# A mixture-of-experts stage: weights in three groups of four parts, and scatters without order

## The chip, the cores and the metric

One core of a Trainium2 chip runs the whole program. The metric is the device time of one execution in microseconds (us); lower is better. The engines are TensorE (PE, with its weight loads shown as PEld), VectorE (DVE), ScalarE (ACT), GpSimd (POOL) and SyncE (SP, which here only issues DMAs).

## What is computed

A sliding-window attention, a gated feed-forward layer and a routed mixture of experts follow one another over 2304 tokens of 512 channels. The change touches the last one only:

```python
def _moe2_ref(x, w_skip, w_gate, w1, w2):          # w1 (8, 512, 1024), w2 (8, 1024, 512)
    out = x.copy()
    do_compute = x @ w_skip > 0
    xc = x[do_compute]
    ...                                            # e_idx: best expert of a token; gate_w: its softmax share
    for e in range(8):
        mask = e_idx == e
        h = np.maximum(xc[mask] @ w1[e], 0.0)
        y[mask] = gate_w[mask, None] * (h @ w2[e])
    out[do_compute] = xc + y
    return out
```

## The kernel before

**Stages.** Attention and the first feed-forward layer run over five blocks of tokens. As each block ends, its tokens go to DRAM (`x1d`, and as a first value to `out`) and are routed. The expert stage, `moe2`, starts when the last block is done, at about 571 us; its first weight loads start at about 545 us.

**Tiles.** Tokens of one expert are gathered in tiles of 128 rows. Each expert has up to two tiles here (s = 0 and 1); whether the second exists is known only on the chip, so PE's work on a second tile stands in a branch (`taken`). With these inputs the experts at places 0, 4 and 6 of the order have a second tile. The largest expert is put first, and one of its tiles is computed early, before the loop (`mm1(0, ...)`, `mm2(0, ...)`, `put(0, ...)`). More tiles than two would run in a loop at the end, which these inputs don't enter.

**Arithmetic.** Products are made in float32r with a high and a low part: each weight part is loaded raw (512 KB), ACT casts the high part (L862, L871), and a subtraction makes the low part (L863 on DVE for w1; L873 for w2, on DVE for parts 1 and 3 and on POOL for parts 2 and 4). Three products for each pair then make 24 matmuls of 512 columns for mm1 (w1) and 24 for mm2 (w2) of one tile.

**One tile's way.** `gather` (POOL) fetches the rows; `tx` turns them on PE into one of two PSUM buffers `tps` and copies them out as `xt`, high part on ACT (L906), low part on DVE (L907); `mm1` fills `hps`; `relu` makes `hr` (half on ACT L918, half on DVE L922); `th` turns `hr` through the same two `tps` buffers and copies it out as `ht` (ACT L933, DVE L934); `mm2` (L943) fills the accumulator `yps[s]`, one for each s; `put` makes `o` on DVE (L949) and scatters its rows into `out` with an indirect DMA that POOL issues (L950). The framework knows only that all scatters write `out`, and keeps them in order: each waits for the one before to land.

**Weights.** An expert's w1 has four parts, and so has its w2. `load_weights(e)` loads all eight, through five raw buffers (`rp`), on SP's queue in the order written. w1 turns in six buffers (`wp1`), w2 in six (`wpx` with two, `wpy` with four): one and a half experts each.

**Order.** Loop round i works on expert e = i: it loads the weights of the next expert, gathers the tokens of the one after, turns the next expert's first tile, does mm1 of e, then mm2 of the expert before (`last`), with transposes between. So mm2 of an expert runs one round after its mm1. The framework's planner then orders the instructions of every engine anew, by the order written and by when it expects their inputs; a branch moves only as a whole. Each engine then works through its queue strictly in that order.

**Memory.** The pools of `moe2` lie over those of the stage before, whose buffers come free one after the other until that stage ends.

Of the kernel before, what the change touches and what calls it, by code (L numbers as in the profile page):

```python
# [8 lines left out]
F32R = mybir.dt.float32r  # L9
# [6 lines left out]
P = 128  # L16
# [810 lines left out]
def moe2(ctx, tc, ph, ps_a, ctab, ident, x1d, ls, cnt, perm, permi, slot0, xg0, w1, w2, out):  # L827
    nc = tc.nc
    NT, DM = out.shape
    KD = DM // P  # L830
    FF = w1.shape[2]
# [12 lines left out]
    def pool(name, bufs, space=None):  # L844
        kw = {"space": space} if space else {}
        return ctx.enter_context(tc.tile_pool(name=name, bufs=bufs, reuse_waits="tile", **kw))

    wp1, rp, wpx, wpy = pool("wp1", 6), pool("rp", 5), pool("wpx", 2), pool("wpy", 4)
    xtp, mt, xp, hp_ = pool("xtp", 3), pool("mt", 1), pool("xp2", 2), pool("hp2", 2)
    n_w2 = [0]  # L850
    ps_h0 = pool("ps_h0", 1, bass.MemoryType.PSUM)
    ps_t = pool("ps_t", 1, bass.MemoryType.PSUM)
    ps_y = [pool(f"ps_y{s}", 1, bass.MemoryType.PSUM) for s in range(2)]
    ps_h1 = pool("ps_h1", 1, bass.MemoryType.PSUM)

    def load_weights(e):
        r1, r2 = [], []
        for c in range(4):
            raw = rp.tile([P, FF], F32, tag="raw", name="raw1")
            nc.sync.dma_start(out=raw, in_=w1[bass.ds(e, 1), c * P:(c + 1) * P, :].rearrange("o p f -> (o p) f"))  # L860
            w = wp1.tile([P, 2, FF], F32R, tag="w1", name="w1s")
            nc.scalar.copy(out=w[:, 0], in_=raw)  # L862
            nc.vector.tensor_tensor(out=w[:, 1], in0=raw, in1=w[:, 0].bitcast(F32), op=ALU.subtract)  # L863
            r1.append(w)
        for c in range(4):
            raw = rp.tile([P, 2, DM], F32, tag="raw", name="raw2")
            src = w2[bass.ds(e, 1), c * 2 * P:(c + 1) * 2 * P, :]
            nc.sync.dma_start(out=raw, in_=src.rearrange("o (two p) d -> p (o two) d", p=P))
            w = (wpx if n_w2[0] % 6 < 2 else wpy).tile([P, 2, 2, DM], F32R, tag="w2", name="w2s")
            n_w2[0] += 1  # L870
            nc.scalar.copy(out=w[:, 0], in_=raw)  # L871
            eng = nc.gpsimd if c in (1, 3) else nc.vector
            eng.tensor_tensor(out=w[:, 1], in0=raw, in1=w[:, 0].bitcast(F32), op=ALU.subtract)  # L873
            r2.append(w)
        return r1, r2

    hps = [(ps_h0, ps_h1)[s].tile([P, 2, FF // 2], F32, tag="h", name=f"hps{s}") for s in range(2)]
    tps = [ps_t.tile([P, 4, P], F32, tag=f"t{s}", name=f"tps{s}") for s in range(2)]
# [2 lines left out]
    def tp(src, yes=None):  # L881
        ps = tps[n_t[0] % 2]
        n_t[0] += 1
        with yes or ExitStack():
            for c in range(4):
                nc.tensor.transpose(ps[:, c], src[:, c * P:(c + 1) * P], ident)
        return ps
# [15 lines left out]
    def tx(xg, yes=None):  # L903
        ps = tp(xg, yes)
        xt = xtp.tile([P, 2, KD, P], F32R, tag="xt", name="xt")
        tx_last[0] = nc.scalar.copy(out=xt[:, 0], in_=ps)  # L906
        tx_last[1] = nc.vector.tensor_tensor(out=xt[:, 1], in0=ps, in1=xt[:, 0].bitcast(F32), op=ALU.subtract)  # L907
        return xt

    def mm1(s, xt, w, hs=(0, 1)):  # L910
        for h in hs:
            for n, (c, a, b) in enumerate(ORDER1):
                nc.tensor.matmul(hps[s][:, h], lhsT=xt[:, a, c], rhs=w[c][:, b, h * 512:(h + 1) * 512],  # L913
                                 start=(n == 0), stop=(n == 3 * KD - 1))

    def relu(s, both=False):
        hr = hp_.tile([P, 2, FF // 2], F32, tag="hr", name="hr")
        nc.scalar.activation(out=hr[:, 0], in_=hps[s][:, 0], func=AF.Relu)  # L918
        if both:
            nc.scalar.activation(out=hr[:, 1], in_=hps[s][:, 1], func=AF.Relu)  # L920
        else:
            nc.vector.tensor_scalar(out=hr[:, 1], in0=hps[s][:, 1], scalar1=0.0, scalar2=None, op0=ALU.max)  # L922
        return hr

    def th(hr, yes=None):
        pss = []
        with yes or ExitStack():
            for h in range(2):
                pss.append(tp(hr[:, h]))
        ht = hp_.tile([P, 2, KF, P], F32R, tag="ht", name="ht", bufs=3)  # L930
        for h in range(2):
            ps = pss[h]
            nc.scalar.copy(out=ht[:, 0, 4 * h:4 * h + 4], in_=ps)  # L933
            nc.vector.tensor_tensor(out=ht[:, 1, 4 * h:4 * h + 4], in0=ps,  # L934
                                    in1=ht[:, 0, 4 * h:4 * h + 4].bitcast(F32), op=ALU.subtract)
        return ht

    def mm2(s, ht, w, cs=range(8)):
        n = 3 * cs[0]
        for c0 in range(cs[0], cs[-1], 4):  # L940
            for a, b in PASSES:
                for c in range(c0, c0 + 4):
                    nc.tensor.matmul(yps[s], lhsT=ht[:, a, c], rhs=w[c // 2][:, b, c % 2],  # L943
                                     start=(n == 0), stop=(n == 3 * KF - 1))
                    n += 1

    def put(s, xg, slot):
        o = hp_.tile([P, DM], F32, tag="o", name="o", bufs=4)
        nc.vector.scalar_tensor_tensor(out=o, in0=yps[s], scalar=slot[2], in1=xg, op0=ALU.mult, op1=ALU.add)  # L949
        nc.gpsimd.indirect_dma_start(  # L950
            out=out, out_offset=bass.IndirectOffsetOnAxis(ap=slot[1].bitcast(U32), axis=0),
            in_=o, in_offset=None, bounds_check=NT - 1, oob_is_err=False)

    def slot_at(i):
        return gi[:, i:i + 1], si[:, i:i + 1], ls[:, 1, i:i + 1]

    wts, xg, xt, hr, ht = {}, {}, {}, {}, {}
    def expert(i):
        return nc.values_load(permi[0:1, i:i + 1], engines=(ET.SP,), min_val=0, max_val=NE - 1,
                              skip_runtime_bounds_check_because="an index of an expert")  # L960

    wts[0] = load_weights(expert(0))
    mm1(0, tx(xg0), wts[0][0])
    mm2(0, th(relu(0, True)), wts[0][1])
    put(0, xg0, slot0)

    gi = mt.tile([P, SLOTS], I32, name="gi")
# [22 lines left out]
    def taken(e, s):  # L990
        return tc.If(tiles_of[e] > 1) if s else ExitStack()

    def stage_g(e):
        for s in range(2):
            if (e, s) in slots:
                xg[e, s] = gather(slots[e, s], f"{e}_{s}")

    def stage_x(e, s):
        if (e, s) in slots:
            xt[e, s] = tx(xg[e, s], taken(e, s) if TX else None)  # L1000

    def stage_1(e, s, hs=(0, 1)):
        if (e, s) in slots:
            with taken(e, s):
                mm1(s, xt[e, s], wts[e][0], hs)
            if hs[-1] == 1:
                hr[e, s] = relu(s)

    def stage_t(e, s):
        if (e, s) in slots:  # L1010
            ht[e, s] = th(hr[e, s], taken(e, s) if TH else None)

    def stage_2(e, s, cs=range(8)):
        if (e, s) in slots:
            with taken(e, s):
                mm2(s, ht[e, s], wts[e][1], cs)
            if cs[-1] == 7:
                put(s, xg[e, s], slots[e, s])

    order = [*range(NE), None, None]  # L1020
# [3 lines left out]
    with tc.issue_after(si_last.ins):  # L1024
# [10 lines left out]
        le = mt.tile([1, 2, NU, NE], F32, name="le")  # L1035
# [26 lines left out]
    last = None  # L1062
    for i, e in enumerate(order[:-1]):
        nxt = order[i + 1]
        if i == 0:
            with tc.issue_after(tx_last[0].ins), tc.issue_after(tx_last[1].ins):
                wts[nxt] = load_weights(expert(nxt))
        elif nxt is not None:
            wts[nxt] = load_weights(expert(nxt))
        stage_g(order[i + 2] if i + 2 < len(order) else None)  # L1070
        if nxt is None:
            stage_1(e, 0)
            stage_t(last, 1)
            stage_1(e, 1)
            stage_2(last, 0, range(4))
            stage_t(e, 0)
            stage_2(last, 0, range(4, 8))
            stage_t(e, 1)
            stage_2(last, 1)
            stage_2(e, 1)  # L1080
            stage_2(e, 0)
            break
        stage_x(nxt, 0)
        stage_1(e, 0, (0,))
        stage_1(e, 1)
        stage_t(last, 1)
        stage_1(e, 0, (1,))
        stage_2(last, 0, range(4))
        stage_x(nxt, 1)
        stage_2(last, 0, range(4, 8))  # L1090
        stage_t(e, 0)
        stage_2(last, 1)
        last = e
    with tc.If(n_extra > 0):
        with tc.For_i(0, n_extra) as u:
            le, la = extra_regs(bass.ds(u, 1), (ET.SP,), (ET.DVE,))
            lw = load_weights(le)
            lslot = pick(la)
            lx = gather(lslot, "loop")
            lxt = tx(lx)  # L1100
            mm1(0, lxt, lw[0])
            lht = th(relu(0))
            mm2(0, lht, lw[1])
            put(0, lx, lslot)


_OUT = (2304, 512)
# [33 lines left out]
```

## Time and profile before

| | |
|---|---|
| time, median of 3 runs | 758.83 us (758.09 to 758.84) |
| time of the profiled execution | 758.27 us |
| its span | 756.5 us |
| PE busy | 715.5 us (95%) |
| DVE busy | 503.5 us (67%) |
| ACT busy | 327.3 us (43%) |
| POOL busy | 86.4 us (11%) |
| raw expert weights | 64 loads of 512 KB, 5.0 us from issue to landing (median) |

The span runs from the first to the last instruction that the profile shows; the time has some 1.8 us around it. Busy time is that of an engine at work on data; waiting, branching and issuing is not counted. Where an engine sat idle before an instruction, the profile names what ended that: the instruction, or the DMA, that released it.

### The profile page before, as it was taken

Reading aid. Unit: us, or ns where it says so; the run is one execution under the profiler, and the core shown is the slowest. Engines: PE = TensorE matmul, PEld = TensorE weight load, DVE = VectorE, ACT = ScalarE, POOL = GpSimd, SP = SyncE. Lnnn points to the kernel's source line nnn. Section 1 sums busy time; section 2 is a strip of 40 time slices with the busy share of each in tenths; the row PEclk is TensorE's granted clock in tenths of the full one; section 3 lists DMA queues with packets and bytes.
Section 4 is the critical chain, followed back from the end, with each engine's and each line's share of the span. In section 5 each row is a group of like instructions: output and inputs, shape, how many; then the busy total and the mean of one; then the engine's idle time right before and its main releaser. Section 6 shows DMA issues by size and latency. Waiting matters only on the chain. (4 is left out here: it accounts for less than half of the span.)

```text
span 756.5 us, 12268 instructions
## 1 busy us (share of the span) xinstructions
PE 715.5 (95%) x4456; PEld 580.6 (77%) x4456; DVE 503.5 (67%) x1122; ACT 327.3 (43%) x758; POOL 86.4 (11%) x65
## 2 busy tenths in 40 slices
PE   6699999999999999999999999999989999899994
PEld 4587778788878787878887888889887777677772
DVE  3988899858944549954457963523865676876662
ACT  5858667634333143233233213212143366765550
POOL 2100000000000000000000000000011416545342
PEclk9999999999999999999999999999999999999998
DMA  9795878775432416414416311116394667967531
GB/s 230 184 229 169 243 236 263 218 219 186 112 99 71 112 58 194 111 56 112 112 57 193 100 56 56 57 58 221 113 396 146 208 196 231 300 229 260 176 134 42
DMA packets 118163, 121.85 MB, mean 161 GB/s; under 512 B 76463, under 2 KB 89135, under 8 KB 118098
## 3 DMA queue, kind: packets, MB, share of 16 engines
q1 hardware_dynamic: 113794, 108.32, 47.9%
q0 software_dynamic: 2720, 6.92, 2.8%
q10 hardware_dynamic: 1584, 5.77, 2.1%
q8 instruction: 38, 0.62, 0.3%
q14 instruction: 27, 0.22, 0.1%
HBM read 102.78 MB, written 20.20 MB: 163 GB/s over the span
## 5 line engine op out<-in xcount | busy, mean ns | idle before, releaser
L411 PE MATMUL po<-wo,h 128*128 128x512 f32 x648 | 160.6, 392 | 2.2 <-DMA wo<-wo_hl 2.2
L387 PE MATMUL g<-xh,wgv 128*128 128x512 f32 (+1 forms) x496 | 152.3, 373 | 4.0 <-DVE th L393 2.2
L387 PE MATMUL v<-xh,wgv 128*128 128x512 f32 (+1 forms) x496 | 149.9, 368 | 0.0
L411 PEld LDWEIGHTS po<-wo,h 128*128 128x128 f32 x648 | 120.5, 188 | 27.2 <-issue 2.5
L387 PEld LDWEIGHTS g<-xh,wgv 128*128 128x128 f32 x496 | 89.9, 188 | 24.0 <-DVE th L393 4.0
L387 PEld LDWEIGHTS v<-xh,wgv 128*128 128x128 f32 x496 | 90.0, 189 | 14.0
L387 PE MATMUL g<-xl,wgv 128*128 128x512 f32 (+1 forms) x248 | 90.2, 364 | 0.9 <-DVE xl L282 0.9
L387 PE MATMUL v<-xl,wgv 128*128 128x512 f32 (+1 forms) x248 | 90.3, 364 | 0.0
L399 ACT CAST h<-th 128x512 fp32r<-128x512 f32 (+1 forms) x62 | 35.2, 567 | 112.0 <-DVE th L397 112.0
L913 PE MATMUL hps<-w1s,xt 128*128 128x512 f32 x288 | 76.1, 404 | 3.9 <-DVE w1s L863 2.6
L392 ACT ACTIVATE th<-g 128x512 f32<-128x512 f32 (+1 forms) x62 | 33.7, 544 | 102.8 <-PE g L387 99.1
L469 DVE SCALAR_TENSOR_TENSOR junk<-x,wrow 128x512 f32<-128x512 f32 x108 | 74.4, 689 | 2.7 <-DMA wrow<-wrow_d 0.5
L943 PE MATMUL yps<-w2s,ht 128*128 128x512 f32 x288 | 73.0, 401 | 2.0 <-DVE o L949 0.9
L393 DVE SCALAR_TENSOR_TENSOR th<-th,g 128x512 f32<-128x512 f32 (+1 forms) x62 | 38.1, 614 | 51.0 <-ACT th L392 50.7
L943 PEld LDWEIGHTS yps<-w2s,ht 128*128 128x128 f32 x288 | 53.1, 188 | 16.1 <-issue 2.5
L913 PEld LDWEIGHTS hps<-w1s,xt 128*128 128x128 f32 x288 | 51.6, 188 | 17.3 <-DVE w1s L863 4.7
L397 DVE SCALAR_TENSOR_TENSOR th<-th,v 128x512 f32<-128x512 f32 (+1 forms) x62 | 38.1, 615 | 35.1 <-PE v L387 34.4
L644 POOL DMA_INDIRECT xge<-x1d,ei x1 | 1.4, 1450 | 521.8 <-DVE th L393 521.8
L400 DVE TENSOR_TENSOR h<-th,h 128x512 fp32r<-128x512 f32 (+1 forms) x62 | 40.2, 649 | 19.3 <-ACT h L399 19.2
L387 PEld LDWEIGHTS g<-xl,wgv 128*128 128x128 f32 x248 | 46.8, 189 | 8.2 <-DVE xl L282 1.3
L387 PEld LDWEIGHTS v<-xl,wgv 128*128 128x128 f32 x248 | 46.8, 189 | 6.6
L873 POOL TENSOR_TENSOR w2s<-raw,w2s 128x1024 fp32r<-128x1024 f32 x16 | 39.7, 2482 | 83.4 <-ACT w2s L871 83.3
(210 smaller groups left out, 972.4 us busy)
## 6 DMA issues: line engine op xcount, KB each, us to landing
raw<-in_moe_w_dram SPq DMA_DIRECT2D x64, 512.0 KB, 5.0
wo<-wo_hl SPq DMA_DIRECT2D x37, 512.0 KB, 3.3
raw<-in_moe_w_gate_dram SPq DMA_DIRECT2D x12, 512.0 KB, 4.2
raw<-in_moe_w_val_dram SPq DMA_DIRECT2D x12, 512.0 KB, 4.6
raw<-in_moe_w_out_dram SPq DMA_DIRECT2D x12, 512.0 KB, 3.4
wo_hl<-wo SPq DMA_DIRECT2D x12, 512.0 KB, 4.0
wo<-wo_hl ACTq DMA_DIRECT2D x11, 512.0 KB, 4.1
x1d<-x SPq DMA_DIRECT2D x18, 256.0 KB, 4.9
```

The costliest lines, as they stand in the source:

```text
L387: nc.tensor.matmul(mm, lhsT=w[:, 2 * m + a, c * P:(c + 1) * P], rhs=x_cols(xs[b], j, c, c0, c1), start=(i == 0), stop=(i == 3 * KD - 1))
L392: nc.scalar.activation(out=th, in_=acc, func=AF.Tanh, scale=0.5)
L393: nc.vector.scalar_tensor_tensor(out=th, in0=th, scalar=1.0, in1=acc, op0=ALU.add, op1=ALU.mult)
L397: nc.vector.scalar_tensor_tensor(out=th, in0=th, scalar=0.5, in1=acc, op0=ALU.mult, op1=ALU.mult)
L399: nc.scalar.copy(out=h[:, 0], in_=th)
L400: (nc.gpsimd if False else nc.vector).tensor_tensor(out=h[:, 1], in0=th, in1=h[:, 0].bitcast(F32), op=ALU.subtract)
L411: nc.tensor.matmul(po[j, i], lhsT=h[:, a, i * P - c0:(i + 1) * P - c0], rhs=wo[:, b], start=(po_n[j, i] == 1), stop=(po_n[j, i] == 3 * NF))
L469: nc.vector.scalar_tensor_tensor(out=junk, in0=x1s[i], scalar=1.0, in1=wrow[0][:, e], op0=ALU.mult, op1=ALU.mult, accum_out=L[:, i, e:e + 1])
L644: nc.gpsimd.indirect_dma_start(out=xge, out_offset=None, in_=x1d[0:BO[-1], :], in_offset=bass.IndirectOffsetOnAxis(ap=ei[:, 0:1].bitcast(m ...
L873: eng.tensor_tensor(out=w[:, 1], in0=raw, in1=w[:, 0].bitcast(F32), op=ALU.subtract)
L913: nc.tensor.matmul(hps[s][:, h], lhsT=xt[:, a, c], rhs=w[c][:, b, h * 512:(h + 1) * 512], start=(n == 0), stop=(n == 3 * KD - 1))
L943: nc.tensor.matmul(yps[s], lhsT=ht[:, a, c], rhs=w[c // 2][:, b, c % 2], start=(n == 0), stop=(n == 3 * KF - 1))
```

## The change

Three things are done in `moe2`.

The weight buffers become three groups of four, `wg0`, `wg1` and `wg2`, each for one w1 or one w2 of one expert. `load_weights` is split in `load_w1` and `load_w2`, and these are called where a group comes free: the w2 of e after the mm1 of e, into the group of its own w1; the w1 of the expert after next at the end of the round, into the group of the w2 whose mm2 has just been written. At the start w1 of the first expert has group 0, its w2 group 1, and w1 of the second group 2.

Scatters of the tiles outside the final loop are declared free of each other, since no two write the same row.

In the last round the mm2 of the next to last expert's second tile is written ahead of that of its first tile.

```diff
-    wp1, rp, wpx, wpy = pool("wp1", 6), pool("rp", 5), pool("wpx", 2), pool("wpy", 4)
+    wg0, wg1, rp, wg2 = pool("wg0", 4), pool("wg1", 4), pool("rp", 5), pool("wg2", 4)
+    wg = wg0, wg1, wg2
...
-    def load_weights(e):
-        r1, r2 = [], []
+    def load_w1(e, g):
+        ws = []
         for c in range(4):
             raw = rp.tile([P, FF], F32, tag="raw", name="raw1")
             nc.sync.dma_start(out=raw, in_=w1[bass.ds(e, 1), c * P:(c + 1) * P, :].rearrange("o p f -> (o p) f"))
-            w = wp1.tile([P, 2, FF], F32R, tag="w1", name="w1s")
+            w = wg[g].tile([P, 2, FF], F32R, tag="w", name="w1s")
             nc.scalar.copy(out=w[:, 0], in_=raw)
             nc.vector.tensor_tensor(out=w[:, 1], in0=raw, in1=w[:, 0].bitcast(F32), op=ALU.subtract)
...
+    def load_w2(e, g):
+        ws = []
         for c in range(4):
             raw = rp.tile([P, 2, DM], F32, tag="raw", name="raw2")
...
-            w = (wpx if n_w2[0] % 6 < 2 else wpy).tile([P, 2, 2, DM], F32R, tag="w2", name="w2s")
+            w = wg[g].tile([P, 2, 2, DM], F32R, tag="w", name="w2s")
...
-    def put(s, xg, slot):
+    def put(s, xg, slot, apart=True):
...
+        if apart:
+            tc.declare_no_dep(d.ins, group="put", reason="other rows")
+            tc.add_to_no_dep_group("put", d.ins)
...
+    reg = {0: expert(0)}
+    g1 = {0: 0, 1: 2, 2: 0}
+    g2 = {0: 1}
+    w1_, w2_ = {0: load_w1(reg[0], 0)}, {0: load_w2(reg[0], 1)}
...
         if i == 0:
             with tc.issue_after(tx_last[0].ins), tc.issue_after(tx_last[1].ins):
-                wts[nxt] = load_weights(expert(nxt))
-        elif nxt is not None:
-            wts[nxt] = load_weights(expert(nxt))
+                reg[nxt] = expert(nxt)
+                w1_[nxt] = load_w1(reg[nxt], g1[nxt])
...
             stage_1(e, 0)
             stage_t(last, 1)
             stage_1(e, 1)
+            stage_2(last, 1)
             stage_2(last, 0, range(4))
             stage_t(e, 0)
             stage_2(last, 0, range(4, 8))
             stage_t(e, 1)
-            stage_2(last, 1)
             stage_2(e, 1)
             stage_2(e, 0)
...
         stage_1(e, 0, (1,))
+        if i:
+            g2[e] = g1[e]
+            w2_[e] = load_w2(reg[e], g2[e])
+        else:
+            reg[far] = expert(far)
+            w1_[far] = load_w1(reg[far], g1[far])
         stage_2(last, 0, range(4))
         stage_x(nxt, 1)
         stage_2(last, 0, range(4, 8))
         stage_t(e, 0)
         stage_2(last, 1)
+        if i and far is not None:
+            g1[far] = g2[last]
+            reg[far] = expert(far)
+            w1_[far] = load_w1(reg[far], g1[far])
+        elif i:
+            g2[nxt] = g2[last]
+            w2_[nxt] = load_w2(reg[nxt], g2[nxt])
```

## Rows read from the trace of the kernel before

**Rows 1.** Busy time by stretch: bounds, length, PE, PEld, DVE, ACT, POOL, clock, DMA.
```profile
642.00:657.00 15.00, 13.45 (x65) 10.29 (x64) 13.24 (x16) 11.71 (x16) 9.39 (x7) 1.00 0.89 295
...
717.00:746.00 29.00, 26.11 (x122) 20.29 (x121) 17.99 (x22) 12.91 (x19) 12.23 (x7) 1.00 0.32 108
```

**Rows 2.** PE's waits from 590 us on: us in total, times, the longest.
```profile
PE hps L913 <- DVE w1s L863: 2.6, 3, 1.7
...
PE tps L886 <- ACT hr L918: 1.3, 1, 1.3
PE tps L886 <- DVE xt L907: 1.1, 1, 1.1
PE yps L943 <- DVE o L949: 0.9, 1, 0.9
...
PE hps L913 <- DVE xt L907: 0.6, 1, 0.6
```

**Rows 3.** Timeline of ACT and PE at four waits: start, length, instructions, idle before.
```profile
606.36 1.04 ACT L871 CAST w2s<-raw 128x1024 fp32r<-128x1024 f32 x1
...
607.95 0.66 PE L886 MATMUL tps<-ctab,hr 128*128 128x128 f32 x4 [1.28 <-ACT hr L918]
...
645.05 0.66 PE L886 MATMUL tps<-ctab,hr 128*128 128x128 f32 x4 [1.10 <-DVE xt L907]
...
681.63 2.81 PE L913 MATMUL hps<-w1s,xt 128*128 128x512 f32 x11 [0.63 <-DVE w1s L863]
...
720.88 0.97 PE L913 MATMUL hps<-w1s,xt 128*128 128x512 f32 x3 [1.65 <-DVE w1s L863]
```

**Rows 4.** Timeline of DVE and POOL at the end of the stage.
```profile
739.38 0.75 DVE L949 SCALAR_TENSOR_TENSOR o<-yps,lst,xg 128x512 f32<-128x512 f32 x1 [1.25 <-PE yps L943]
...
742.98 0.75 DVE L949 SCALAR_TENSOR_TENSOR o<-yps,lst,xg 128x512 f32<-128x512 f32 x1 [0.94 <-PEq L1015]
746.55 0.75 DVE L949 SCALAR_TENSOR_TENSOR o<-yps,lst,xg 128x512 f32<-128x512 f32 x1 [2.82 <-PE yps L943]
...
740.41 1.00 POOL L950 DMA_INDIRECT out_dram<-o,si  x1 [3.43 <-DVE o L949]
...
748.02 0.97 POOL L950 DMA_INDIRECT out_dram<-o,si  x1 [2.43 <-DVEq L1094]
750.89 0.97 POOL L950 DMA_INDIRECT out_dram<-o,si  x1 [1.89 <-issue]
```

**Rows 5.** Timeline of PE at the end of the stage.
```profile
728.25 7.42 PE L943 MATMUL yps<-w2s,ht 128*128 128x512 f32 x31
...
740.28 6.24 PE L943 MATMUL yps<-w2s,ht 128*128 128x512 f32 x24 [0.94 <-DVE o L949]
```

**Rows 6.** Instructions of the tiles w1s and w2s: ns shortest/median/longest, first and last start.
```profile
L862 ACT CAST w1s<-raw x32: 1039/1050/1062, 549.7 to 719.9; 128x1024 fp32r<-128x1024 f32 x32
L863 DVE TENSOR_TENSOR w1s<-raw,w1s x32: 1209/1222/2672, 551.2 to 722.5; 128x1024 fp32r<-128x1024 f32 x32
...
L873 POOL TENSOR_TENSOR w2s<-raw,w2s x16: 2378/2471/2679, 561.8 to 734.5; 128x1024 fp32r<-128x1024 f32 x16
```

**Rows 7.** Timeline of POOL and DVE ahead of two of the waits.
```profile
676.88 2.49 POOL L873 TENSOR_TENSOR w2s<-raw,w2s 128x1024 fp32r<-128x1024 f32 x1 [4.80 <-ACT w2s L871]
...
677.78 2.67 DVE L863 TENSOR_TENSOR w1s<-raw,w1s 128x1024 fp32r<-128x1024 f32 x1
...
717.14 2.61 POOL L873 TENSOR_TENSOR w2s<-raw,w2s 128x1024 fp32r<-128x1024 f32 x1 [3.28 <-ACT w2s L871]
...
718.35 2.48 DVE L863 TENSOR_TENSOR w1s<-raw,w1s 128x1024 fp32r<-128x1024 f32 x1
```

**Rows 8.** PE's waits from 545 to 590 us: us in total, times, the longest.
```profile
PE po L411 <- DMA wo<-wo_hl: 2.2, 2, 1.2
```

**Rows 9.** Timeline of SP: two groups of raw loads, start and length.
```profile
626.36 9.50 SPq L860 DMA_DIRECT2D raw<-in_moe_w_dram  x4
...
654.52 4.91 SPq L868 DMA_DIRECT2D raw<-in_moe_w_dram  x4
```

More of the change, by code (lines that the diff above doesn't have):

```diff
@@ L846, in pool @@
         return ctx.enter_context(tc.tile_pool(name=name, bufs=bufs, reuse_waits="tile", **kw))
-    wp1, rp, wpx, wpy = pool("wp1", 6), pool("rp", 5), pool("wpx", 2), pool("wpy", 4)
+    wg0, wg1, rp, wg2 = pool("wg0", 4), pool("wg1", 4), pool("rp", 5), pool("wg2", 4)
+    wg = wg0, wg1, wg2
     xtp, mt, xp, hp_ = pool("xtp", 3), pool("mt", 1), pool("xp2", 2), pool("hp2", 2)
-    n_w2 = [0]
     ps_h0 = pool("ps_h0", 1, bass.MemoryType.PSUM)
@@ L860, in load_weights @@
             nc.sync.dma_start(out=raw, in_=w1[bass.ds(e, 1), c * P:(c + 1) * P, :].rearrange("o p f -> (o p) f"))
-            w = wp1.tile([P, 2, FF], F32R, tag="w1", name="w1s")
+            w = wg[g].tile([P, 2, FF], F32R, tag="w", name="w1s")
             nc.scalar.copy(out=w[:, 0], in_=raw)
             nc.vector.tensor_tensor(out=w[:, 1], in0=raw, in1=w[:, 0].bitcast(F32), op=ALU.subtract)
-            r1.append(w)
+            ws.append(w)
+        return ws
+    def load_w2(e, g):
+        ws = []
         for c in range(4):
@@ L868, in load_weights @@
             nc.sync.dma_start(out=raw, in_=src.rearrange("o (two p) d -> p (o two) d", p=P))
-            w = (wpx if n_w2[0] % 6 < 2 else wpy).tile([P, 2, 2, DM], F32R, tag="w2", name="w2s")
-            n_w2[0] += 1
+            w = wg[g].tile([P, 2, 2, DM], F32R, tag="w", name="w2s")
             nc.scalar.copy(out=w[:, 0], in_=raw)
@@ L873, in load_weights @@
             eng.tensor_tensor(out=w[:, 1], in0=raw, in1=w[:, 0].bitcast(F32), op=ALU.subtract)
-            r2.append(w)
-        return r1, r2
+            ws.append(w)
+        return ws
     hps = [(ps_h0, ps_h1)[s].tile([P, 2, FF // 2], F32, tag="h", name=f"hps{s}") for s in range(2)]
@@ L945, in mm2 @@
                     n += 1
-    def put(s, xg, slot):
+    def put(s, xg, slot, apart=True):
         o = hp_.tile([P, DM], F32, tag="o", name="o", bufs=4)
         nc.vector.scalar_tensor_tensor(out=o, in0=yps[s], scalar=slot[2], in1=xg, op0=ALU.mult, op1=ALU.add)
-        nc.gpsimd.indirect_dma_start(
+        d = nc.gpsimd.indirect_dma_start(
             out=out, out_offset=bass.IndirectOffsetOnAxis(ap=slot[1].bitcast(U32), axis=0),
             in_=o, in_offset=None, bounds_check=NT - 1, oob_is_err=False)
+        if apart:
+            tc.declare_no_dep(d.ins, group="put", reason="other rows")
+            tc.add_to_no_dep_group("put", d.ins)
     def slot_at(i):
         return gi[:, i:i + 1], si[:, i:i + 1], ls[:, 1, i:i + 1]
-    wts, xg, xt, hr, ht = {}, {}, {}, {}, {}
+    xg, xt, hr, ht = {}, {}, {}, {}
     def expert(i):
@@ L960, in expert @@
                               skip_runtime_bounds_check_because="an index of an expert")
-    wts[0] = load_weights(expert(0))
-    mm1(0, tx(xg0), wts[0][0])
-    mm2(0, th(relu(0, True)), wts[0][1])
+    reg = {0: expert(0)}
+    g1 = {0: 0, 1: 2, 2: 0}
+    g2 = {0: 1}
+    w1_, w2_ = {0: load_w1(reg[0], 0)}, {0: load_w2(reg[0], 1)}
+    mm1(0, tx(xg0), w1_[0])
+    mm2(0, th(relu(0, True)), w2_[0])
     put(0, xg0, slot0)
@@ L1004, in stage_1 @@
             with taken(e, s):
-                mm1(s, xt[e, s], wts[e][0], hs)
+                mm1(s, xt[e, s], w1_[e], hs)
             if hs[-1] == 1:
@@ L1015, in stage_2 @@
             with taken(e, s):
-                mm2(s, ht[e, s], wts[e][1], cs)
+                mm2(s, ht[e, s], w2_[e], cs)
             if cs[-1] == 7:
@@ L1064, in moe2 @@
         nxt = order[i + 1]
+        far = order[i + 2] if i + 2 < len(order) else None
         if i == 0:
             with tc.issue_after(tx_last[0].ins), tc.issue_after(tx_last[1].ins):
-                wts[nxt] = load_weights(expert(nxt))
-        elif nxt is not None:
-            wts[nxt] = load_weights(expert(nxt))
+                reg[nxt] = expert(nxt)
+                w1_[nxt] = load_w1(reg[nxt], g1[nxt])
         stage_g(order[i + 2] if i + 2 < len(order) else None)
@@ L1096, in moe2 @@
             le, la = extra_regs(bass.ds(u, 1), (ET.SP,), (ET.DVE,))
-            lw = load_weights(le)
+            lw = load_w1(le, 0), load_w2(le, 1)
             lslot = pick(la)
@@ L1103, in moe2 @@
             mm2(0, lht, lw[1])
-            put(0, lx, lslot)
+            put(0, lx, lslot, False)
 _OUT = (2304, 512)
```

## The prediction

> **What bounds the kernel now.** I read the busy time by stage first. The change lies in the last stage, from about 545 us on; there TensorE (PE) is the long pole: 13.45 of 15.00 us in a round with one token tile, 26.11 of 29.00 us in the last stretch, at full clock, while VectorE (DVE) and ScalarE (ACT) stay below it [rows 1]. So a gain must be idle time of PE in this stage, or time behind PE's last matmul. The list of PE's waits gives the first kind: 2.6 us in three waits for a w1 remainder (the subtraction at L863), 1.1 and 0.6 us for the turned tokens xt (L907), 1.3 us for a ReLU (L918), 0.9 us for an output row block o (L949) [rows 2]. The timeline of PE gives their places: 1.28 us before 607.95, 1.10 before 645.05, 0.63 before 681.63, 1.65 before 720.88 [rows 3]. The second kind is at the end: DVE finishes the last o at 746.55 + 0.75 = 747.30, but GpSimd (POOL) starts its scatter only at 750.89; the last scatters, at 740.41, 748.02 and 750.89 among them, are some 3 us apart although each is about 1 us of POOL [rows 4].
>
> **Part 1, scatters free of each other.** Before, a scatter into out waits until the one before has landed. The first of the four, at 740.41, followed its o (739.38 + 0.75 = 740.13) by 0.28 us; nothing was in flight ahead of it that it still had to wait for. The last one came 3.59 us behind its o [rows 4]. With the dependency gone it can start at 747.30 + 0.28 = 747.58 instead of 750.89: **3.3 us**, all of it on the path, because what stands behind the last scatter (its descriptors, its landing, the drain) is unchanged and merely moves. The scatters ahead of it have their o by 742.98 + 0.75 = 743.73, and are out of the way at 1 us each. Bounds: 0 if a wait remains, 3.3 if none does; I take 3.3, since the row of 740.41 shows a scatter without one. In the middle of the stage the same waits cost PE nothing now, and removing them only lets POOL reach its weight subtractions sooner.
>
> **Part 2, three groups of four.** Before, w1 turns in six buffers and w2 in six. Parts 3 and 4 of the next expert's w1 can be converted only after this expert's mm1, and must be ready one mm2 later: 24 matmuls, 6.24 us [rows 5]. In that window stand their casts (1.05 us each), their subtractions (1.22 us), and those of the w2 parts ahead of them in the same queues, where POOL takes 2.47 us for each of its two [rows 6]. That is where PE's waits come from: the ReLU of 607.95 stood on ACT behind a w2 cast that ran at 606.36 [rows 3], and the subtractions that ended the waits of 681.63 and 720.88 took 2.67 and 2.48 us, not 1.22: they ran beside a POOL subtraction (676.88 to 679.37, 717.14 to 719.75) and ended 1.08 us behind its end each time [rows 7].
>
> After, a w2 is loaded into the group of its own expert's w1, from the end of mm1 on, and is read after the mm2 of the last expert and the mm1 of the next: two passes, 12.5 us. The w1 of the expert after next goes into the group that mm2 has left, a whole round ahead of its use. The longest work on a w2 group is two casts, then two POOL subtractions one after the other: 2 x 1.05 + 2 x 2.47 = 7.0 us [rows 6], so at least 5.4 us are spare; a w1 group (4 x 1.05 + 1.22 = 5.4 us) has more. None of the waits for w1 should stay (2.6 us), and the waits for xt and ReLU that came from conversions ahead of them in ACT's and DVE's queues should mostly go (1.1 + 0.6 + 1.3): **5.6 us**. Bounds: 0 (each is replaced by another) to 5.6; I take all of it here and book what comes back apart.
>
> What comes back: four casts of a w2 come free at once, when mm1 ends. Behind them on ACT stand the copies of xt and of the hidden layer ht; behind the subtractions on DVE stand the other half of these copies and the o's; PE's next transposes need the two PSUM buffers that these copies clear. There are seven such groups (experts 1 to 7). If none delays PE the price is 0; if each costs what the xt wait costs (1.10 us [rows 3]) it is 7.7 us. The delayed piece is now a w2 part with 5 us to spare, not what PE reads next, so I stay near the lower end: 0.3 us each, **2 us** back.
>
> The subtractions of w2 parts 2 and 4 keep their place on POOL, but move behind the gathers of that round and stay ahead of the scatters of the last expert; gathers are read a round later, scatters by nobody. On SP the raw loads keep their number and size; only their order changes, and one register load per expert stays. The groups also lie elsewhere over the memory of the stage before: all of the first w2 now lies on buffers that are free when it arrives, so its conversion and the raw loads of the next w1 come earlier, beside loads of wo for which PE waits 2.2 us [rows 8]. That can move these waits either way, by -2.2 to +2.2 us; with no reason for a sign I take 0. The early expert's own first pass needs nothing of it sooner.
>
> **Part 3, second tile of the next to last expert first.** The source changes, but PE's order is the planner's. Before, 31 matmuls run in a row from 728.25 on, which is more than the 24 of a whole pass, and the last pass waits 0.94 us at 740.28 for the o that clears its accumulator [rows 5]. That accumulator is tile 0's; had the second tile stood between, as the source has it, that o would have been long done. So I read it that the planner had already put the second tile ahead of tile 0's second half. After, tile 0's second half is again directly ahead of the last pass, so this wait stays. **0 us**; bounds -0.9 (the wait goes) and +1.1 (the second tile starts before its ht is copied and waits as at 645.05 [rows 3]).
>
> **Sum.** -3.3 - 5.6 + 2.0 = -6.9 us against the profiled execution, 758.27 us (span 756.5): **751.4 us**. The median of the runs, 758.83, is 0.56 us above that execution, and its runs reach from 758.09 to 758.84, so I leave the sum as it is.
>
> **Rivals.** (a) Slower: the burst. Each w2 group puts POOL's two subtractions beside DVE's two, and DVE then stands as in rows 7, with xt, ht and o behind it. If PE pays each of seven times what it paid at 720.88 (1.65 us), that is 11.6 us against 8.9 gained: 758.27 + 2.7 = 761.0. It decides from 8.9 / 7 = 1.27 us per group on. For it: all three wait places above show DVE late. Against: what stood behind then was a w1 that PE read at once. The Trainium skill, page "SBUF — State Buffer", section "Who interferes with whom", has this as a rule: a DVE instruction with two SBUF inputs and a GpSimd instruction that reads SBUF exclude each other, and the later one waits until the other has finished. The trace agrees (ends 1.08 us behind POOL's end, rows 7); by that rule the lengthening comes with every w2 group, which is this rival's condition, but not that PE pays for it. Chance 0.07.
>
> (b) The waits are replaced one for one, by other copies late on ACT; only the tail is won: 758.27 - 3.3 = 755.0. For it: waits for xt come from queue order, which every new plan draws anew. Chance 0.17.
>
> (c) Supply. SP needed from 626.36 to 654.52 for three groups, 28.2 us, or 9.4 us a group [rows 9]. A round with one tile is 15 us [rows 1] and needs two groups, 18.8 us. Over two such rounds 7.6 us are missing, of which 5.4 are spare: PE waits 2.2 us or more, 753.6 to 759. Against: before, part of those 9.4 us was waiting for buffers that the change frees. Chance 0.09, some 755.
>
> (d) The scatters don't come free (another wait holds them): 758.27 - 5.6 + 2.0 = 754.7. Chance 0.05.
>
> **How the numbers follow.** The forecast has 0.62, its own range 748.5 to 753.5. The range for eight in ten takes in (b), (d) and most of (c), and below it the best case, all 8.9 us won and 1 us of the unknown terms: 748.0 to 757.0. A measurement of this kernel tells about 0.2%, 1.5 us, from no change. Faster by more than that: forecast, (b), (d) and most of (c), 0.88, less a margin for a plan that I can't see: 0.86. Within it: what is left of (c) and that margin, 0.07. Slower: (a), 0.07.
>
> **What would show it.** Part 1: the last scatter starts within 0.4 us of its o's end, and the last four no longer 3 us apart. Part 2: no PE wait for L863 in the list, and no wait over 1 us between 606 and 740; DVE subtractions of 2.5 us may still occur, on w2. Part 3: a wait of some 0.9 us ahead of the last 24 matmuls. Rival (a) would show as waits for xt or ht in every round, (c) as PE or ACT waiting for raw loads between 630 and 660. The forecast is wrong if the last matmul, at 746.5 before, ends later than 745.

## The result and the profile after

| | before | after |
|---|---|---|
| time, median | 758.84 us (758.09 to 763.76) | 752.41 us (750.75 to 754.78) |
| time of the profiled execution | 758.27 us | 750.75 us |
| its span | 756.5 us | 748.9 us |
| PE, DVE, ACT, POOL busy | 715.5, 503.5, 327.3, 86.4 us | 713.7, 505.8, 326.5, 86.0 us |

The ratio after to before is 0.990, with a 95% interval of 0.988 to 0.993. The forecast was 751.4 us (748.0 to 757.0), faster. The work is the same; what went is waiting.

PE's waits from 590 us on in the kernel after: us in total, times, the longest. They answer to [rows 2].

```profile
PE yps L947 <- DVE o L953: 1.2, 1, 1.2
PE hps L917 <- PE hps L917: 1.2, 1, 1.2
PE tps L890 <- DVE ht L938: 1.1, 2, 0.9
PE tps L890 <- DVE xt L911: 1.0, 1, 1.0
...
PE tps L890 <- ACT hr L922: 0.3, 1, 0.3
```

No wait for a remainder of w1 is left, and the ReLU's is 0.3 instead of 1.3 us. The list has a new name, ht, and a wait whose releaser is an instruction of PE itself (hps behind hps). Their places are in the timeline of PE (start, length, instructions, idle time before and what ended it):

```profile
592.82 0.66 PE L890 MATMUL tps<-ctab,xg 128*128 128x128 f32 x4 [0.96 <-DVE xt L911]
...
594.87 11.23 PE L917 MATMUL hps<-w1s,xt 128*128 128x512 f32 x47 [1.16 <-PE hps L917]
...
606.86 0.66 PE L890 MATMUL tps<-ctab,hr 128*128 128x128 f32 x4 [0.33 <-ACT hr L922]
...
644.43 0.60 PE L890 MATMUL tps<-ctab,xg 128*128 128x128 f32 x4
...
689.35 0.66 PE L890 MATMUL tps<-ctab,xg 128*128 128x128 f32 x4 [0.90 <-DVE ht L938]
...
736.09 0.93 PE L947 MATMUL yps<-w2s,ht 128*128 128x512 f32 x3 [1.16 <-DVE o L953]
```

The reader is to hold these against [rows 3]: the transposes that waited 1.28 us at 607.95 wait 0.33 now, those of 645.05 (1.10 us) start at 644.43 without a wait. Busy time by stretch, as in [rows 1], shows the same from the other side: in the round of 15 us PE is busy for 14.55 us where it was 13.45.

```profile
642.00:657.00 15.00, 14.55 (x70) 11.17 (x69) 12.84 (x16) 11.18 (x16) 10.56 (x7) 1.00 0.81 277
```

At the end, POOL and DVE (timeline, as [rows 4]):

```profile
736.21 0.97 POOL L954 DMA_INDIRECT out_dram<-o,si  x1 [3.07 <-DVE o L953]
738.17 0.97 POOL L954 DMA_INDIRECT out_dram<-o,si  x1 [0.98 <-DVE o L953]
743.38 0.97 POOL L954 DMA_INDIRECT out_dram<-o,si  x1 [4.24 <-DVEq L1118]
```

```profile
735.20 0.74 DVE L953 SCALAR_TENSOR_TENSOR o<-yps,lst,xg 128x512 f32<-128x512 f32 x1
...
737.15 0.75 DVE L953 SCALAR_TENSOR_TENSOR o<-yps,lst,xg 128x512 f32<-128x512 f32 x1 [0.61 <-PEq L1026]
742.35 0.75 DVE L953 SCALAR_TENSOR_TENSOR o<-yps,lst,xg 128x512 f32<-128x512 f32 x1 [4.46 <-PE yps L947]
```

Each of these scatters now starts 0.27 to 0.28 us behind the end of its o: 735.94 and 736.21, 737.90 and 738.17, 743.10 and 743.38.

**Where the time went.** From PE's last matmul to the start of the last scatter it was 750.89 - 746.51 = 4.38 us and is 743.38 - 742.31 = 1.07 us: -3.3 us. PE's last matmul ends 4.2 us earlier (746.51 to 742.31). Together that is 7.5 of the span's 7.6 us. From the start of the last scatter to the end of the span it is 5.6 us before and after, so that the tail behind it only moved. Of the 4.2 us, 0.86 lie ahead of the first mm2 (585.95 and 585.09) and 3.35 behind it: that stretch is 160.57 us before and 157.22 after.

A second profile of the change, taken with the experiments (`after_again`), has a stretch of 154.52 us. PE's waits from 590 us on add up to 5.8 us in the first profile and to 3.5 in the second: there the 1.16 us ahead of the mm1 and the 0.90 us for ht are missing. So rows of 1 us in a single profile of the change are not all the change's.

### The profile page after: what moved, and what is told of

Read it like the earlier page. It is cut to its first block, busy times and chain, and to the rows that moved or that the text cites. A ratio compares the mean times of both kernels' runs of the same rounds, so it can differ in the third digit from the quotient of the medians.

```text
span 748.9 us, 12262 instructions
## 1 busy us (share of the span) xinstructions
PE 713.7 (95%) x4456; PEld 581.0 (78%) x4456; DVE 505.8 (68%) x1122; ACT 326.5 (44%) x758; POOL 86.0 (11%) x65
## 5 line engine op out<-in xcount | busy, mean ns | idle before, releaser
L917 PE MATMUL hps<-w1s,xt 128*128 128x512 f32 x288 | 73.0, 399 | 1.2 <-PE hps L917 1.2
```

## Experiments

Times are medians; ratios are against the kernel before on the same chip, whose median there was 758.6 to 761.4 us, and a gain in us is the ratio's, of that median. The theory is that of the prediction: a free tail, and w1 buffers that come free a round earlier. "The stage" below is the time from the first matmul of mm2 to the end of the last.

### The parts one by one

Part 1 alone, on the kernel before:

```diff
+        if apart:
+            tc.declare_no_dep(d.ins, group="put", reason="other rows")
+            tc.add_to_no_dep_group("put", d.ins)
```

> The kernel before with part 1 alone: scatters declared free of each other, six and six weight buffers and the old order kept. Theory: only the tail changes, by the 3.3 us between 750.89 and 747.58, so about 755.5 us against 758.8, and the last scatter starts within 0.4 us of its o's end. Rival: freeing the scatters lets the planner draw a new order for the whole stage, and PE's waits between 600 and 746 change by more than 1 us either way, so that the time lies outside 754.5 to 756.5.

Measured: 756.46 us against 759.66, ratio 0.996 (0.994 to 0.998), 2.9 us less. The last scatter on POOL and its o on DVE:

```profile
748.02 0.97 POOL L950 DMA_INDIRECT out_dram<-o,si  x1 [2.59 <-DVE o L949]
```

```profile
746.99 0.75 DVE L949 SCALAR_TENSOR_TENSOR o<-yps,lst,xg 128x512 f32<-128x512 f32 x1 [2.82 <-PE yps L943]
```

The last scatter comes 0.28 us behind its o (747.74), and PE's waits stay as in [rows 2] (w1s 2.6, ReLU 1.3, xt 1.1, o 0.9). The stage is 161.34 us (160.57 before). So part 1 is the tail and nothing else.

Part 2 alone: the change with the scatters in order, and the last round as before.

```diff
-        if apart:
+        if False:
             tc.declare_no_dep(d.ins, group="put", reason="other rows")
```

> The kernel before with part 2 alone: three groups of four in the new load order, scatters still in order, last round as before. Theory: the waits for w1 go, PE's last matmul ends some 3 to 4 us earlier, and the tail of serial scatters stays: 755 to 756 us against 758.8. Rival b of the prediction: the waits are replaced by others, within 1 us of 758.8.

Measured: 756.31 us, ratio 0.996 (0.994 to 0.999), 3.0 us less (3.6 expected). No wait for w1; the stage is 157.12 us. The scatters are a chain again; the one ahead of the last starts at 746.06:

```profile
748.93 0.97 POOL L954 DMA_INDIRECT out_dram<-o,si  x1 [1.90 <-DMA out_dram<-o,si]
```

The last o ends at 745.25, so 3.68 us of the tail are unused. POOL's wait names the landing of the scatter ahead as its releaser, which the trace of before did not.

Parts 1 and 2 without part 3:

```diff
-            stage_2(last, 1)
             stage_2(last, 0, range(4))
             stage_t(e, 0)
             stage_2(last, 0, range(4, 8))
             stage_t(e, 1)
+            stage_2(last, 1)
```

> The changed kernel with part 3 undone (last round in the old order). Theory: PE's order stays the same but for a few matmuls of the last pass, and with free scatters nothing waits for the earlier output: 752.4 us, within 0.5 us of the changed kernel. Rival: the reorder is worth the wait of the last pass, and without it the time is 1 us longer or shorter.

Measured: 751.71 us, ratio 0.991 (0.988 to 0.994), which is the change's own ratio; the stage is 155.43 us, and the last pass waits 0.94 us for its o. The two parts add up (2.9 + 3.0 against 7.0 us, within the intervals), and part 3 on top of them is worth nothing that the times show.

Part 3 alone, the same edit the other way round, on the kernel before:

> The kernel before with part 3 alone. Theory of the prediction: 0 us, since PE's order hardly changes, 758.8. Rival: while scatters wait for each other, part 3 lets the second tile's scatter go ahead of the last three, so that the chain of scatters at the end is one shorter, 2.9 us (from 748.02 to 750.89): 755.9 us.

Measured: 755.53 us, ratio 0.995 (0.992 to 0.998), 4.0 us less: the 0 us of the theory missed, and the rival with a shorter tail hit. (Only the end of its profile is read: that execution took 759.49 us, with a granted clock of 0.96 from 610 to 650 us and a stage of 163.85 us.) The last two scatters on POOL and the last two o on DVE there:

```profile
749.13 0.97 POOL L950 DMA_INDIRECT out_dram<-o,si  x1 [3.06 <-DMA out_dram<-o,si]
752.13 0.97 POOL L950 DMA_INDIRECT out_dram<-o,si  x1 [2.02 <-DVE o L949]
```

```profile
746.60 0.75 DVE L949 SCALAR_TENSOR_TENSOR o<-yps,lst,xg 128x512 f32<-128x512 f32 x1 [0.68 <-PEq L1015]
751.10 0.75 DVE L949 SCALAR_TENSOR_TENSOR o<-yps,lst,xg 128x512 f32<-128x512 f32 x1 [3.75 <-PE yps L943]
```

The third o ends at 747.35 and its scatter still waits for a landing until 749.13; but the last o ends at 751.85, later than that scatter's landing, and its scatter follows after 0.28 us. The last four o's start over 10.85 us here (740.25 to 751.10) and over 7.17 before (739.38 to 746.55 [rows 4]), so that the chain has caught up by the end: of the last four scatters one waits for a landing here, three before. Parts 1 and 3 win the same 3 us of tail; that is why part 3 adds nothing behind part 1. The last pass waits its 0.94 us in this kernel too.

### What comes back: the exclusion of DVE and POOL

Rival (a) of the prediction says that POOL's subtractions on w2 lengthen DVE's, and that PE pays. If so, POOL should not have them at all. On the kernel before, and on the kernel after:

```diff
-            eng = nc.gpsimd if c in (1, 3) else nc.vector
+            eng = nc.vector
```

> The kernel before with all subtractions of w2 on DVE, none on POOL. Theory: two of the three waits for w1 (before 681.63 and 720.88, 0.63 and 1.65 us) came from DVE standing still beside a POOL subtraction; without these no DVE subtraction takes over 1.3 us, those waits shrink, and the time falls by 1 to 2.3 us, to 756.5 to 757.8, although DVE has 14 subtractions (17 us) more to do in the stage. Rival: the waits come from DVE's queue being long; with more on it they grow, and the time is 759 us or more.

> The changed kernel with all subtractions of w2 on DVE, none on POOL. Theory: the lengthened DVE subtractions of the changed kernel are on w2 parts with time to spare, so taking them away is worth nothing: 752.4, within 0.7 us. Rival a of the prediction (POOL beside DVE costs PE time in every round): 1 us or more faster. If DVE is near its limit in rounds with one tile: 1 us or more slower.

Measured: 767.84 us, ratio 1.007 (1.005 to 1.010), on before; 766.06 us, ratio 1.005 (1.002 to 1.008), on after, where the change itself is at 0.990. No subtraction is lengthened any more, and still both are slower. PE's waits in the first:

```profile
PE hps L913 <- DVE hr L922: 3.7, 4, 1.1
PE tps L886 <- DVE ht L934: 3.4, 4, 1.5
PE tps L886 <- DVE xt L907: 1.7, 2, 1.0
```

and in the second:

```profile
PE tps L890 <- DVE ht L938: 7.0, 5, 2.0
```

The w1 wait is gone even on before, as expected, but the copies hr, ht and xt now stand behind 16 more subtractions of 1.22 us on DVE. Both theories missed, and the rivals of a DVE queue too long came true. So POOL's share is worth more than its exclusion costs; what the lengthening itself costs can't be read here, since DVE has 16 x 1.22 = 19.5 us more to do. The rows show PE waiting for a PSUM copy late in DVE's queue.

The waits are not the whole loss. On before, the stage is 170.16 us, 9.6 longer, while PE's waits from 590 us on add up to 12.9 us instead of 8.7. Here the clock granted to PE fell, to 0.91 from 650 to 690 us and 0.93 from 720 to 745, where before has 1.00: an estimate of 0.09 x 40 + 0.07 x 25 = 5.4 us from these rows, which is the rest. On after, the stage is 169.72 us, 12.5 longer, the waits 9.6 more (15.4 to 5.8); the clock is 0.91 from 590 to 610 us and 0.93 from 720 to 745, some 3.6 us by the same estimate.

### What comes back: supply of raw weights

Rival (c) says that raw loads come too late. ACT's waits in the kernel after, from 590 us on, bear it out in kind: 15.2 us for raw weights, where before had 4.9.

```profile
ACT w2s L875 <- DMA raw<-in_moe_w_dram: 10.9, 10, 2.5
...
ACT w1s L863 <- DMA raw<-in_moe_w_dram: 4.3, 4, 1.5
```

And one of them explains the wait of PE at 689.35 in this profile. ACT, then DVE, of the kernel after:

```profile
687.04 1.06 ACT L875 CAST w2s<-raw 128x1024 fp32r<-128x1024 f32 x1 [2.51 <-DMA raw<-in_moe_w_dram]
687.99 1.06 ACT L937 CAST ht<-tps 128x512 fp32r<-128x512 f32 x2
```

```profile
688.60 1.29 DVE L938 TENSOR_TENSOR ht<-tps,ht 128x512 fp32r<-128x512 f32 x2 [1.24 <-ACT ht L937]
```

A w2 cast stood at the head of ACT's queue and waited 2.51 us for its raw load; the two ht copies, whose input was ready, stood behind it; DVE's ht followed at 688.60, and PE had waited 0.90 us. In the second profile of the change the same cast waits 0.99 us for its load, and PE starts that transpose without a wait, though ACT waits 13.3 us for raw weights in all. To take the supply wait away, seven raw buffers instead of five:

```diff
-    wg0, wg1, rp, wg2 = pool("wg0", 4), pool("wg1", 4), pool("rp", 5), pool("wg2", 4)
+    wg0, wg1, rp, wg2 = pool("wg0", 4), pool("wg1", 4), pool("rp", 7), pool("wg2", 4)
```

> The changed kernel with seven raw buffers for five. Theory: raw loads are not what PE waits for: 752.4, within 0.7 us. Rival c (supply): loads run further ahead and the time falls by 1 to 2 us, with a smaller spread between runs if it is late loads that make the runs differ by 4 us.

Measured: 764.51 us, ratio 1.002 (0.999 to 1.005), where the change itself is at 0.990: a loss, where the supply theory has a gain. The run does not answer the question, since something else changed with it. Its SP queue at the start of the weights, and then that of the kernel after:

```profile
546.27 1.72 SPq L861 DMA_DIRECT2D raw<-in_moe_w_dram  x2
...
573.64 1.08 SPq L861 DMA_DIRECT2D raw<-in_moe_w_dram  x2
```

```profile
544.42 2.06 SPq L861 DMA_DIRECT2D raw<-in_moe_w_dram  x4
```

The third raw load, which starts right behind the first two in the kernel after, starts only at 573.64, behind the last writes of the stage before, and the first matmul of mm2 at 595.04 instead of 585.09. That the larger pool lies on memory that this stage still uses is the likely reason; it was not shown apart. Behind that point the stage itself is 163.51 us, with only 4.5 us of ACT's waits for raw weights: so it grew with the supply mended, as in the run that follows. The same buffers without that confusion are two extra ones in a pool of their own behind the others, used from the 17th load on:

```diff
+    rq, n_raw = pool("rq", 2), [0]
+
+    def raw_pool():
+        n_raw[0] += 1
+        return rq if n_raw[0] > 16 and n_raw[0] % 7 in (0, 3) else rp
...
-            raw = rp.tile([P, FF], F32, tag="raw", name="raw1")
+            raw = raw_pool().tile([P, FF], F32, tag="raw", name="raw1")
```

(and the same for raw2), beside the change itself once more on that chip:

> The changed kernel with two more raw buffers that lie apart and serve only loads from the second expert's w2 on, so that nothing changes for the first sixteen loads. Theory: in the changed kernel ACT waits 15.2 us in 14 places for raw loads, but PE pays only where a copy of ht stands behind such a cast (0.9 us before 689.35); with loads further ahead ACT's waits halve at least and the time falls by 0.5 to 1 us. Rival c of the prediction (supply sets the pace of the rounds with one tile): 2 us or more faster. Rival: the casts come in bursts whatever the loads do, and then POOL's and DVE's subtractions meet more often: no gain, or slower.

> The changed kernel itself, beside the two that follow on one chip. Theory: 0.990 of the kernel before, as at first (0.988 to 0.993).

Measured: 757.48 us, ratio 0.999 (0.996 to 1.001), against 752.21 us, ratio 0.991 (0.988 to 0.993), for the change. The supply is mended, ACT waits for raw weights 5.0 us instead of 15.2, and the kernel is 5.3 us slower: the theory missed, and the rival of bursts came true. PE's waits in it:

```profile
PE tps L895 <- DVE ht L943: 4.8, 4, 2.0
PE tps L895 <- DVE xt L916: 1.7, 2, 1.0
```

The longest of them, at 675.17, in the timelines of POOL, DVE and PE of that kernel:

```profile
667.66 2.43 POOL L882 TENSOR_TENSOR w2s<-raw,w2s 128x1024 fp32r<-128x1024 f32 x1 [5.07 <-ACT w2s L880]
670.87 2.56 POOL L882 TENSOR_TENSOR w2s<-raw,w2s 128x1024 fp32r<-128x1024 f32 x1 [0.78 <-ACT w2s L880]
```

```profile
664.35 6.82 DVE L869 TENSOR_TENSOR w1s<-raw,w1s 128x1024 fp32r<-128x1024 f32 x4
...
672.30 2.22 DVE L882 TENSOR_TENSOR w2s<-raw,w2s 128x1024 fp32r<-128x1024 f32 x1
674.44 1.27 DVE L943 TENSOR_TENSOR ht<-tps,ht 128x512 fp32r<-128x512 f32 x2
```

```profile
675.17 0.66 PE L895 MATMUL tps<-ctab,xg 128*128 128x128 f32 x4 [2.00 <-DVE ht L943]
```

The four w1 subtractions take 6.82 us instead of 4 x 1.22 = 4.9 (the last one is blocked by POOL's of 667.66), and the w2 subtraction 2.22 instead of 1.22: it ends at 674.52, 1.09 us behind POOL's end (670.87 + 2.56 = 673.43). Behind it stands ht, behind ht PE. In the stage 13 of DVE's 48 subtractions are lengthened, by 15.7 us in all; in the kernel after, 5, by 5.5 us. With weights on hand the conversions of a group run as one burst on DVE and POOL at once. So rival (a)'s mechanism is real, in a kernel where PE's ht and xt waits are 4.8 + 1.7 us; in the kernel after, the late raw loads spread the conversions out.

The Trainium skill, page "SBUF — State Buffer", section "Who interferes with whom", states the exclusion of such DVE and GpSimd instructions (two inputs in SBUF on DVE, a read of SBUF on GpSimd); the lengthening seen here, up to POOL's end and 1.09 us more, agrees.

Here too the clock adds to the waits. Busy time in one stretch behind the wait of 675.17 (columns as in [rows 1]), and the timeline of PE there:

```profile
678.00:680.00 2.00, 1.85 (x6) 0.96 (x5) 1.96 (x4) 1.78 (x2) 1.02 (x1) 0.50 0.98 337
```

```profile
676.51 3.28 PE L922 MATMUL hps<-w1s,xt 128*128 128x512 f32 x8
...
681.95 3.00 PE L922 MATMUL hps<-w1s,xt 128*128 128x512 f32 x12
```

Behind the wait the granted clock is 0.77 from 676 to 678 us, 0.50 (1.2 GHz) to 680, and 1.00 again from 682 on: 8 matmuls take 3.28 us, 0.41 each, where later 12 take 3.00, 0.25 each. The stage is 162.12 us, 4.9 or 7.6 longer than in the two profiles of the change; PE's waits from 590 us on add up to 9.2 us, 3.4 or 5.7 more. The rest, 1.5 or 1.9 us, is about what the lower clock costs.

Is the lengthening itself what PE pays? The same split of work, but with POOL on parts 3 and 4, where fewer DVE subtractions stand beside it (with the last pass in another accumulator, as below):

```diff
-            eng = nc.gpsimd if c in (1, 3) else nc.vector
+            eng = nc.gpsimd if c in (2, 3) else nc.vector
```

> The changed kernel with the last pass in a free PSUM bank (as a_last_acc) and with POOL taking parts 3 and 4 of each w2 for its subtractions in place of 2 and 4, so that DVE's two come ahead of POOL's two and not between them. Theory: a DVE subtraction that meets a POOL one stands still until that has ended, so the five lengthened DVE subtractions (5.5 us in all) become two or fewer, and with them PE's waits for ht: 0.985 to 0.988 of the kernel before, at or below a_last_acc (0.9887). Rival: POOL's two now run back to back into the next group's w1, whose subtractions are lengthened in their place: the same sum of lengthening, and 1 us or more slower than a_last_acc.

Measured: 753.12 us, ratio 0.992 (0.989 to 0.995). The theory missed (0.985 to 0.988), but the interval overlaps that of the run it builds on (0.986 to 0.991). Only 2 subtractions of DVE are lengthened, by 1.2 us, as expected, but PE waits no less:

```profile
PE tps L890 <- DVE ht L938: 1.9, 2, 1.1
PE tps L890 <- DVE xt L911: 1.8, 2, 1.0
```

With most of DVE's lengthening taken away the waits for ht and xt stay. That points to the place of these copies in ACT's and DVE's queues, rather than the length of what stands ahead, for the waits of 1 us that are left. It is not shown for the waits of 2 us with the extra buffers, where 2.9 us of lengthening stood ahead of the ht: that kernel without the exclusion was not run.

### The wait ahead of the last pass

The last pass waits for the o that clears yps[0]. By then hps[0] is free, so the last pass can go there:

```diff
-            stage_2(e, 0)
+            stage_2(e, 0, acc=hps[0][:, 0])
```

> The changed kernel with the last pass (mm2 of the last expert's first tile) accumulating in the first mm1 bank of PSUM, which is free by then, in place of the accumulator that the pass before it uses. Theory: the wait of 1.16 us at 736.09 for the o that clears the accumulator goes, and the time is 1.1 us shorter, 751.3. Rival: the last pass then waits as long for its own ht, and the time stays at 752.4.

> Both the two extra raw buffers and the last pass in a free PSUM bank. Theory: the sum of the two, 1.1 us for the last pass and 0.5 to 1 us for the loads: 1.6 to 2.1 us below the changed kernel. Rival: only the last pass counts, 1.1 us below.

Measured for the first: 752.64 us, ratio 0.989 (0.986 to 0.991). The wait is gone; PE runs into the last 24 matmuls without idle time:

```profile
737.24 6.17 PE L947 MATMUL hps<-w2s,ht 128*128 128x512 f32 x24
```

Its ratio is the lowest of all, but its interval lies over those of the change (0.990 and 0.991), so that a gain of 1 us over the change is shown in the row, not in the time. The second, this edit with the two extra raw buffers, took 758.13 us, ratio 0.997 (0.994 to 1.000), with the ht and xt waits of the extra buffers (4.8 and 1.7 us) and no wait for o: both the theory and its rival, each a gain over the change, missed, and the loss through the buffers is not mended by it.

## Why the prediction was right

**Part 1** was predicted at -3.3 us and is -3.3 us in the profiles of before and after, -2.9 us (1.4 to 4.4) alone. The reading of [rows 4] carried it: of four scatters one had nothing ahead of it, and followed its o by 0.28 us.

**Part 2** was predicted at -5.6 + 2.0 = -3.6 us, and the stage is 3.35 us shorter in the first profile of the change, 6.05 in the second (154.52), and 3.0 us (1.1 to 4.7) by the time of the part alone. The first term can be seen. Gone are the 2.6 us for w1 [rows 2], 1.0 of the ReLU's 1.3, and the xt waits of 645 and of mm1 (1.1 + 0.6): 5.3 us of 5.6. The mechanism shows too: no w1 subtraction is lengthened any more (the longest took 1.28 us, 2.67 before); the five that are lengthened are on w2, as the prediction allowed. The xt wait that is left, 0.96 us at 592.82, is none of these: it stands at the loop's start, where before waits 1.57 us at 594.27. Back came ht (1.1 us), 0.2 us at the o, and 1.16 us ahead of 594.87: 2.5 us in the first profile, 2.0 predicted. That these two agree is luck. The term was 0.3 us for each of seven groups; of the 2.5 us only the ht wait at 689 is the kind that was booked, a copy behind a conversion, and that conversion was late for its raw load and not through POOL. The 1.16 us are not the change's with any certainty: the second profile of the change has no such row, and the profile of part 3 alone, on the old weights, has one of 1.22. In the second profile 0.2 us of ht and 0.2 at the o are all that came back. So the runs put this term between 0.4 and 2.5 us, and its form, a small price in every group, is not what they show.

Rival (c) was right in its first half (ACT waits 15.2 us for raw weights) and wrong in its price: only one of these waits reaches PE in the first profile and none in the second, and mending them makes the kernel slower. Rival (a) had its condition named rightly, the subtractions beside each other, and its point of decision, 1.27 us per group, isn't reached: with the extra buffers, where it acts in full, PE's ht and xt waits are 6.5 us over seven groups, 0.9 us each, and the whole lengthening of the stage, lower clock and all, 4.9 to 7.6 us, 0.7 to 1.1 us each. The prediction priced a wait at its own length and had no term for the clock that falls behind it; the change itself didn't need one, with 1.00 in its whole stage. Rivals (b) and (d) fell with the waits and with the tail. The early loads of wo, taken at 0 between -2.2 and +2.2, show 2.4 us after and 2.2 before [rows 8].

**Part 3** was predicted at 0 and is 0 within the change. Read as a part alone the step was wrong: it looked only at the wait ahead of the last pass (0.94 us before, 1.16 after; that it stays was right) and not at what the spread of the last o's does to a chain of scatters. The gain of 4.0 us (1.9 to 6.1) alone and that of part 1 are largely one gain, of which the prediction had booked the whole under part 1.

The last matmul ends at 742.31, ahead of the 745 us that were set as the mark. Of the other signs, no wait over 1 us between 606 and 740, the wait at 736.09 (1.16 us) breaks the letter; it is the one that part 3 expected to stay, of some 0.9 us. **Open:** the times of one kernel reach over some 4 us, so that none of the terms below 1 us is shown in a time, only in rows; the 0.86 us ahead of the first mm2 are within what that point moves between executions (585.09 and 587.04 for the change itself). Whether, with the extra buffers, the lengthening or only the order of the burst makes the ht late was not separated. That ht and xt copies put ahead of the conversions would win the rest was not tried.

## What to carry to other kernels

A wait list names who was late; ask whether it was its own length or its place in an in-order queue: here, fewer lengthened subtractions did not help, and a faster supply of weights, which bunched the conversions ahead of the PSUM copies, cost 5 us. Read the granted clock beside the waits: in the kernels that lost, some waits were followed by matmuls at a lower clock, so that the loss was larger than the waits. Read two profiles of a kernel before a row of 1 us is put down to the change. Two changes that each shorten the same tail must not be added: look whether the end waits for a chain or for the last producer, and give the gain to one of them. A larger buffer pool can delay the loads it is to speed up: with seven raw buffers the third load came 28 us later, probably because the pool then lay over memory that the earlier stage still used.

## What the runs showed of the hardware

**The exclusion goes both ways.** With POOL on parts 3 and 4 its own subtractions grow. Its timeline there, two pairs:

```profile
655.29 5.63 POOL L877 TENSOR_TENSOR w2s<-raw,w2s 128x1024 fp32r<-128x1024 f32 x2 [4.47 <-ACT w2s L875]
...
724.50 4.76 POOL L877 TENSOR_TENSOR w2s<-raw,w2s 128x1024 fp32r<-128x1024 f32 x2
```

and DVE's at the first pair:

```profile
655.07 1.21 DVE L877 TENSOR_TENSOR w2s<-raw,w2s 128x1024 fp32r<-128x1024 f32 x1
```

The first pair began 0.22 us into a subtraction of DVE, which kept its 1.21 us, and took 0.87 us more than the second pair, which had no such neighbour. The other pairs of this kernel agree: of its 16 POOL subtractions, seven began inside a w2 subtraction of DVE and took 2.49 to 3.31 us; the other nine took 2.39 to 2.42.

**PE's clock fell where the weights were late.** With seven raw buffers, busy time by stretch (bounds, length, PE, PEld, DVE, ACT, POOL, granted clock, DMA):

```profile
570.00:575.00 5.00, 4.45 (x31) 3.61 (x30) 2.68 (x4) 3.40 (x5) 0.00 (x0) 1.00 0.51 190
575.00:580.00 5.00, 4.16 (x16) 2.54 (x15) 4.01 (x23) 1.49 (x4) 0.00 (x0) 0.66 1.00 326
...
585.00:590.00 5.00, 2.77 (x7) 2.19 (x8) 4.90 (x8) 1.04 (x1) 1.66 (x2) 0.50 0.70 243
```

and PE at its wait for w1:

```profile
587.23 5.74 PE L917 MATMUL hps<-w1s,xt 128*128 128x512 f32 x13 [2.50 <-DVE w1s L864]
```

Until 575 the clock is full (1.00, the level of 2.4 GHz); then PE, which had been busy for 4.45 of 5 us, gets 0.66, and 0.50 (1.2 GHz) in the stretch where it waits for w1. The 13 matmuls behind that wait take 5.74 us, 0.44 us each; in the kernel after, 47 of the same shape take 11.23 us, 0.24 each. In the kernel after the mean clock from 575 to 595 us is 1.00:

```profile
575.00:595.00 20.00, 16.95 (x90) 13.49 (x90) 14.42 (x63) 3.84 (x9) 8.31 (x9) 1.00 0.37 120
```

So the late load cost twice, in waiting and in slower matmuls. The kernels with the extra buffers and with all of w2 on DVE show the same fall behind waits of PE, to 0.50 at 678 us in the first. What of PE's doing let the clock fall is not settled by these runs.
